# A longer hold on TensorE's tiling in a planned kernel of attention and two dense layers

## The chip, the cores and the metric

The kernel runs on one core of a Trainium2 chip. The metric is the device time of one execution in microseconds (us), the median of several runs. Five engines work in parallel, each through its own instructions in a fixed order: TensorE (PE in the profile, with its weight loads as PEld), VectorE (DVE), ScalarE (ACT), GpSimd (POOL) and SyncE (SP), which issues all the transfers.

## The reference, cut to what matters

The sizes are B, H, S, D = 4, 8, 576, 64 and 2304 tokens through two dense layers, 512 to 2048 and back.

```python
scores = scale * np.matmul(q, k.transpose(0, 1, 3, 2))
x = (psi_rel / psi_i)[..., None]          # log distances, one per pair of positions
h = np.maximum(x @ w1 + b1, 0.0)          # 32 hidden units
bias = h @ w2                             # one value per head
scores = scores + bias.transpose(2, 0, 1)[None, :, :, :]
attn = softmax(scores)                    # over the keys
attn_out = np.matmul(attn, v)
x = attn_out.transpose(0, 2, 1, 3).reshape(B * S, H * D)
h = x @ w_in
out = (h / (1 + exp(-h))) @ w_out
```

All is float32; the kernel makes the precision of the large products out of two parts of each operand (`hi` and `lo`) in a shorter format.

## The kernel before, in words

The program is not written as a loop nest that each engine follows. It is a list of operations, each with the engines that may run it, an estimated cost on each, a due time (`prio`), the buffers that it reads and writes, and a function that emits its instructions. The class `Plan` then walks through simulated time (`order`, lines 118 to 212): whenever an engine is free it takes, among the operations that are ready and whose buffers can be had, the one with the smallest due time. The result is a static order for every engine, and the program emits it. Due times are counted in the plan's own microseconds; they only rank the work.

The work comes in stages that overlap:

- The bias of each pair of positions is computed once for all batches, in 36 tiles (`bias_tile`, line 311): four operations `bias_f` on ScalarE, VectorE or GpSimd (lines 326 and 328), one product `bias_mm` on TensorE (line 334, eight or sixteen matmuls in a 128x32 tiling), one scaling copy `bias_ev` (lines 341 and 343) and a store (line 345). Tiles are due 2.6 apart.
- Attention runs in visits (`visit`, line 463). A visit is one batch, one pair of heads and one or more chunks of 128 query positions. For each chunk (`chunk`, line 537) there are two score products `s_mm` (line 561; the last, half chunk has one, `s_last`, line 552), a maximum on VectorE with the bias added (line 568), the exponential on ScalarE (line 575), two groups of transposes `t_mm` on TensorE (line 584, four and five matmuls) and their copies `p_ev` into the buffer `pt` (on ScalarE or VectorE by the helper `copy`, lines 270 and 272). When all chunks of the visit are in `pt`, the product `pv` (line 483, 20 matmuls in a 128x64 tiling) multiplies them with the values; its result is copied to `xo` and stored to `x_d` (line 497).
- The first batch is done chunk by chunk, 20 visits of one chunk, due 4.5 apart (3.0 for the half chunk); batches 1, 2 and then 3 follow in 24 visits of two and three chunks.
- The dense layers follow in six blocks of 384 tokens with 16 steps each (`ff_step`, line 627): four products `h_mm` (line 633), the gate on ScalarE and VectorE (lines 638 and 642), three products `out_mm` (line 656). Their due times overlap the last three batches of attention; the first block also splits the weights into two parts (lines 352 to 394).

Buffers are scarce and set the order too: `pt` has two, the transposes' two kinds of banks (`TA`, `TB`) one each, the scores' `S`, the bias products' `B` and the outputs' `o` two each.

On TensorE the planner knows three tilings of the array: 1 for `pv`, 2 for `bias_mm`, 0 (the full array) for all else. The table `MODES` names them, `CHANGE` is the time that it adds to the plan for a change, and `KEEP` is added to the due time of every waiting product of another tiling than the present one, when TensorE chooses (lines 58, 168 to 172 and 184 to 186):

```python
wait[e] = [(p + self.KEEP * (self.MODES.get(self.kinds[i], 0) != mode), p, i) for p, i in every]
```

A product of another tiling is taken as soon as no product of the present tiling that could start has a due time up to KEEP later. Until 24 plan-us short products on zeros fill TensorE's idle time (`warm_up`).

Of the kernel before, what the change touches and what calls it, by code (L numbers as in the profile page):

```python
# [46 lines left out]
class Plan:  # L47
# [7 lines left out]
    CALM = 24.0  # L55


    MODES, CHANGE, KEEP = {"pv": 1, "bias_mm": 2}, 0.19, 1.5
    LAG = {"PE": 0.2, "ACT": 0.15, "DVE": 0.13, "POOL": 0.15, "SP": 0.95}

    def __init__(self, caps, banks):
# [726 lines left out]
```

## Time and profile before

| what | value |
|---|---|
| median of three runs | 736.17 us (735.53 to 736.71) |
| the profiled execution | 736.04 us |
| its span, first to last instruction | 734.3 us |
| granted TensorE clock, mean | 0.998 |
| PE busy | 712.6 us, 97% |
| PEld busy | 590.1 us, 80% |
| DVE busy | 421.0 us, 57% |
| ACT busy | 389.4 us, 53% |
| POOL busy | 281.4 us, 38% |

Busy time is the union of an engine's instructions. Matmuls are pipelined, so what a product costs is read from start to start and not from its own duration. In the timeline, neighbouring instructions of one line on one engine are merged into a row: start, time from the first start to the last end, engine, line, operation, destination and source by the program's names, shape, and the count; in square brackets stands the idle time ahead of it and what ended it. A stretch such as "42 to 84 us" is counted from the span's start.

### The profile page before, as it was taken

The page shows a single profiled execution, that of the slowest core. Times are in us where ns is not written, and L with a number is a line of the kernel's source. Part 1 is how long each engine was busy: PE and PEld are TensorE (multiplying, and loading weights), DVE is VectorE, ACT ScalarE, POOL GpSimd, SP SyncE. Part 2 cuts the span into 40 slices and gives each one's busy share as a digit, 9 for nine tenths or more (in the row PEclk, how much of TensorE's full clock was granted, in tenths as well). Part 3 has the DMA queues.
Part 4 walks back from the last instruction along what each step waited for, and adds up shares of the span by engine and source line. Part 5 has one row for each costly group of instructions (what it writes and reads, how often), then busy time and mean ns, then how long its engine had stood idle before and what let it go on. Part 6 is the DMA issues. An engine that isn't in the chain of part 4 may idle for free.

```text
span 734.3 us, 13019 instructions
## 1 busy us (share of the span) xinstructions
PE 712.6 (97%) x4642; PEld 590.1 (80%) x4642; DVE 421.0 (57%) x862; ACT 389.4 (53%) x820; POOL 281.4 (38%) x277
## 2 busy tenths in 40 slices
PE   9899999999999999989999999999999999999997
PEld 4376698677777787778888888899998999999996
DVE  6999968999999999996553544213211221211111
ACT  8899968886786777765443454222222232222222
POOL 5464524474746445573122251123223322422221
PEclk9999999999999999999999999999999999999999
DMA  6998899898584594879856567736454644346001
GB/s 195 372 315 270 277 310 359 278 289 297 191 290 157 203 303 149 272 257 311 293 165 224 168 217 241 263 115 196 148 162 153 186 150 152 125 136 195 1 0 44
DMA packets 68384, 154.77 MB, mean 211 GB/s; under 512 B 9056, under 2 KB 24032, under 8 KB 68320
## 3 DMA queue, kind: packets, MB, share of 16 engines
q1 hardware_dynamic: 68320, 153.94, 63.7%
q8 instruction: 37, 0.61, 0.4%
q14 instruction: 27, 0.22, 0.1%
HBM read 125.12 MB, written 28.79 MB: 210 GB/s over the span
## 4 chain that ended last, share of the span: by engine, by line
PE 46%; issue 7%; DVE 3%; POOL 2%; DMA 1%; ACT 0%; POOLq 0%; DVEq 0%; ACTq 0%
PE psum L633 18%; PE psum L656 18%; PE psum L483 3%; PE psum L561 3%; PE psum L584 3%; POOL M L275 2%; DVE G L568 1%; DVE w L369 1%; DMA G<-in_k_dram 1%; PE psum L552 1%; DVE M L275 0%; DVE w L374 0%; DVE th L642 0%; DVE M L272 0%; DVE w L360 0%
## 5 line engine op out<-in xcount | busy, mean ns | idle before, releaser
L633 PE MATMUL psum<-M,G 128*128 128x384 f32 x1152 | 238.8, 339 | 1.0 <-POOL M L275 0.8
L656 PE MATMUL psum<-G,M 128*128 128x512 f32 x864 | 238.0, 397 | 1.2 <-DVE M L275 0.9
L633 PEld LDWEIGHTS psum<-M,G 128*128 128x128 f32 x1152 | 203.4, 188 | 16.6 <-POOL M L275 1.0
L275 POOL TENSOR_TENSOR M<-th,M 128x384 fp32r<-128x384 f32 x82 | 84.9, 1035 | 272.0 <-ACT M L270 189.3
L642 DVE SCALAR_TENSOR_TENSOR th<-th,psum 128x384 f32<-128x384 f32 x96 | 53.0, 552 | 216.4 <-ACT th L638 216.4
L656 PEld LDWEIGHTS psum<-G,M 128*128 128x128 f32 x864 | 156.7, 188 | 22.2 <-DVE M L275 1.6
L575 ACT ACTIVATE G<-G,sm 128x576 f32<-128x576 f32 (+1 forms) x144 | 111.8, 777 | 53.6 <-DVE sm L568 52.3
L638 ACT ACTIVATE th<-psum 128x384 f32<-128x384 f32 x96 | 47.1, 491 | 161.1 <-PE psum L633 160.0
L568 DVE CUSTOM_DVE_ANT_0 G<-psum,G 128x576 f32<-128x576 f32 (+1 forms) x144 | 106.5, 758 | 27.9 <-PE psum L561 15.5
L584 PE MATMUL psum<-ident,G 128*128 128x128 f32 x656 | 93.5, 276 | 5.7 <-DVE sm L568 3.3
L561 PE MATMUL psum<-G,M 128*128 128x288 f32 x512 | 90.9, 310 | 4.9 <-DVE sm L568 3.5
L584 PEld LDWEIGHTS psum<-ident,G 128*128 128x128 f32 x656 | 75.3, 141 | 23.0 <-issue 4.8
L561 PEld LDWEIGHTS psum<-G,M 128*128 128x128 f32 x512 | 73.9, 190 | 19.7 <-issue 6.7
L483 PE MATMUL psum<-pt,M 128*64 128x128 f32 (+3 forms) x880 | 87.5, 346 | 1.6 <-DVE sm L568 0.8
L483 PEld LDWEIGHTS psum<-pt,M 128*64 128x64 f32 x880 | 52.1, 137 | 30.7 <-issue 6.8
L270 ACT ACTIVATE pt<-psum 128x512 f32<-128x512 f32 (+3 forms) x111 | 59.4, 551 | 28.1 <-PE psum L584 27.0
L275 POOL TENSOR_TENSOR M<-M 64x256 fp32r<-64x256 f32 (+3 forms) x40 | 48.6, 1217 | 57.9 <-DVE M L272 21.0
L270 ACT ACTIVATE M<-th 128x384 fp32r<-128x384 f32 x81 | 42.3, 523 | 40.9 <-DVE th L642 40.0
L272 DVE COPY pt<-psum 128x512 f32<-128x512 f32 (+3 forms) x81 | 45.4, 571 | 21.8 <-PE psum L584 19.1
L275 POOL TENSOR_TENSOR G<-w,G 128x512 fp32r<-128x512 f32 x25 | 35.6, 1425 | 23.8 <-ACT G L270 19.9
L275 POOL TENSOR_TENSOR G<-G 128x576 fp32r<-128x576 f32 x21 | 32.2, 1540 | 29.6 <-PE psum L334 9.6
L326 ACT ACTIVATE G<-lut_sb,cb 128x528 f32<-128x528 f32 (+16 forms) x71 | 41.6, 662 | 0.0
(55 smaller groups left out, 574.1 us busy)
## 6 DMA issues: line engine op xcount, KB each, us to landing
G<-win_d SPq DMA_DIRECT2D x80, 512.0 KB
G<-bias_d SPq DMA_DIRECT2D x48, 576.0 KB
bias_d<-G SPq DMA_DIRECT2D x36, 295.5 KB
G<-in_k_dram SPq DMA_DIRECT2D x16, 576.0 KB
G<-in_w_in_dram SPq DMA_DIRECT2D x16, 512.0 KB
G<-in_w_out_dram SPq DMA_DIRECT2D x16, 512.0 KB
win_d<-G SPq DMA_DIRECT2D x16, 512.0 KB
M<-in_v_dram SPq DMA_DIRECT2D x16, 320.0 KB
```

The source lines that it names most:

```text
L270: A.activation(out=out, in_=in_, func=AF.Copy)
L272: ENG[e].tensor_copy(out=out, in_=in_)
L275: ENG[e].tensor_tensor(out=out, in0=in0, in1=f(in1), op=ALU.subtract)
L483: T.matmul(out=tl(o)[x, 0:w], lhsT=tl(vs)[:, (s + 1) % 5 * 128 + 64 * a:(s + 1) % 5 * 128 + 64 * a + 64], rhs=tl(pt)[:, s + 5 * a if s < 4 ...
L561: T.matmul(out=s[:, hf, 0:288], lhsT=tl(qs)[:, x0 + 128 * a:x0 + 128 * a + 128], rhs=tl(part)[:, S * a + 288 * hf:S * a + 288 * hf + 288], ...
L568: V.tensor_tensor_reduce(out=mine(p, a).rearrange("p (a n) -> p a n", a=2), in0=tl(sps[a]).rearrange("p (a n) -> p a n", a=2)[:, :, 0:widt ...
L575: A.activation(out=mine(p, a), in_=mine(p, a), func=AF.Exp, scale=-1.0, bias=tl(sm)[:, i + a:i + a + 1], accum_out=tl(sq)[:, 2 * c + a:2 * ...
L584: T.transpose(out=tl(tp)[:, 128 * s:128 * s + 128], in_=tl(p)[:, 128 * (s0 + s):128 * (s0 + s) + 128], identity=ident)
L633: T.matmul(out=tl(hp)[:, 0:TB], lhsT=tl(wr)[:, x, 128 * cc:128 * cc + 128], rhs=tl(xs[cc])[:, y, :], start=(cc + m == 0), stop=(cc == NC - ...
L638: A.activation(out=tl(th), in_=tl(hp)[:, 0:TB], func=AF.Tanh, scale=0.5)
L642: V.scalar_tensor_tensor(out=tl(th), in0=tl(th), scalar=1.0, in1=tl(hp)[:, 0:TB], op0=ALU.add, op1=ALU.mult)
L656: T.matmul(out=tl(acc[i]), lhsT=tl(gg)[:, x, 128 * i:128 * i + 128], rhs=tl(wo[fi])[:, y, :], start=(fi == 0 and m == 0), stop=(fi == NF - ...
```

## The change

One constant of the planner is doubled.

```diff
-    MODES, CHANGE, KEEP = {"pv": 1, "bias_mm": 2}, 0.19, 1.5
+    MODES, CHANGE, KEEP = {"pv": 1, "bias_mm": 2}, 0.19, 3.0
```

TensorE's choice now counts a product of another tiling as due 3.0 plan-us later than it is, where it was 1.5. No operation, cost, due time or buffer changes. Since the planner goes on from each choice, the order of later work on all five engines can differ.

## Rows read from the trace of the kernel before

**Rows 1.** The page's totals: busy us, share of span, instructions of each engine.
```profile
PE 712.6 (97%) x4642; PEld 590.1 (80%) x4642; DVE 421.0 (57%) x862; ACT 389.4 (53%) x820; POOL 281.4 (38%) x277
```

**Rows 2.** Stages: stretch, its us, busy us (instructions) per engine, clock, DMA share, GB/s.
```profile
core 0: us, PE busy (x) PEld busy (x) DVE busy (x) ACT busy (x) POOL busy (x), PEclk, DMA share, GB/s
42.00:84.00 42.00, 42.00 (x446) 27.86 (x445) 38.65 (x102) 40.98 (x90) 20.77 (x16) 1.00 0.86 270
84.00:132.00 48.00, 45.82 (x493) 39.41 (x493) 37.83 (x97) 35.69 (x85) 17.52 (x33) 1.00 1.00 333
132.00:320.00 188.00, 177.50 (x1186) 143.29 (x1183) 182.18 (x334) 141.27 (x295) 101.65 (x87) 1.00 0.71 239
320.00:734.00 414.00, 409.08 (x2239) 359.79 (x2237) 126.94 (x265) 137.00 (x286) 117.35 (x117) 1.00 0.52 170
```

**Rows 3.** Timeline of TensorE: products with and without a change of tiling beside them.
```profile
60.77 0.77 PE L561 MATMUL psum<-G,M 128*128 128x288 f32 x4
61.48 1.31 PE L483 MATMUL psum<-pt,M 128*64 128x128 f32 x20
...
97.86 0.77 PE L561 MATMUL psum<-G,M 128*128 128x288 f32 x4
98.47 0.71 PE L584 MATMUL psum<-ident,G 128*128 128x128 f32 x5
...
100.88 1.31 PE L483 MATMUL psum<-pt,M 128*64 128x128 f32 x20
102.12 1.20 PE L584 MATMUL psum<-ident,G 128*128 128x128 f32 x9
103.08 1.30 PE L561 MATMUL psum<-G,M 128*128 128x288 f32 x8
...
104.86 2.40 PE L483 MATMUL psum<-pt,M 128*64 128x128 f32 x40
107.19 1.20 PE L584 MATMUL psum<-ident,G 128*128 128x128 f32 x9
...
152.47 1.15 PE L584 MATMUL psum<-ident,G 128*128 128x128 f32 x9
153.37 1.53 PE L561 MATMUL psum<-G,M 128*128 128x288 f32 x8
```

**Rows 4.** Timeline of TensorE from 48 to 55 us.
```profile
48.02 1.31 PE L483 MATMUL psum<-pt,M 128*64 128x128 f32 x20
49.26 0.66 PE L584 MATMUL psum<-ident,G 128*128 128x128 f32 x4
49.85 1.31 PE L483 MATMUL psum<-pt,M 128*64 128x128 f32 x20
51.09 0.77 PE L334 MATMUL psum<-G,cb 128*32 128x336 f32 x8
51.79 0.77 PE L584 MATMUL psum<-ident,G 128*128 128x128 f32 x5
...
53.55 1.42 PE L334 MATMUL psum<-G,cb 128*32 128x352 f32 x16
54.90 1.31 PE L483 MATMUL psum<-pt,M 128*64 128x128 f32 x20
```

**Rows 5.** Timeline of TensorE from 68 to 73 us.
```profile
68.39 1.31 PE L483 MATMUL psum<-pt,M 128*64 128x128 f32 x20
69.64 0.66 PE L584 MATMUL psum<-ident,G 128*128 128x128 f32 x4
70.22 0.99 PE L334 MATMUL psum<-G,cb 128*32 128x464 f32 x8
71.14 0.77 PE L584 MATMUL psum<-ident,G 128*128 128x128 f32 x5
71.83 1.31 PE L483 MATMUL psum<-pt,M 128*64 128x128 f32 x20
```

**Rows 6.** Timeline of ScalarE: two copies of transposes into the probabilities' buffer.
```profile
47.68 0.71 ACT L270 ACTIVATE pt<-psum 128x640 f32<-128x640 f32 x1
...
65.27 1.19 ACT L270 ACTIVATE pt<-psum 128x512 f32<-128x512 f32 x2
```

## The prediction, made before the changed kernel ran

> **What bounds the kernel now.** I read the profile in this order: the engines' totals, the same engines by stage, then TensorE's timeline inside the stages where the change can act. The totals say that TensorE has matmuls in flight for 712.6 of 734.3 us [rows 1]; the profiled execution took 736.04 us, 1.7 us more than its span and 0.13 us under the median of the runs (736.17), so I work on 736.04 and add 0.13 at the end. The stages say more [rows 2]. From 42 to 84 us TensorE never pauses, but ScalarE is busy for 40.98 of 42.00 us and VectorE for 38.65: three engines are full together. From 84 to 132 us TensorE is the fullest (45.82 of 48.00) and the others have room (VectorE 37.83, ScalarE 35.69), while the DMA share is 1.00. From 132 to 320 us VectorE sets the pace, 182.18 of 188.00 us, and TensorE is idle for 10.5 us. From 320 us on TensorE is alone and full, 409.08 of 414.00 us. So a microsecond of TensorE work that is saved is worth a microsecond at the end after 320 us, nearly that between 84 and 132 us, only in part between 42 and 84 us, and little between 132 and 320 us.
>
> **What the change acts on.** The constant KEEP is added, in the planner's choice for TensorE, to the due time of every waiting product whose tiling is not the one that the array has (lines 168 to 172). Full 128x128 products are tiling 0, the probability-times-value products (`pv`, line 483, 128x64) tiling 1, the bias products (`bias_mm`, line 334, 128x32) tiling 2. The first bias products ended by 90 us and the last `pv` by 467 us, so nothing after that is ordered by it. No instruction is added or removed; what can change is how often TensorE leaves the full tiling and comes back, and in what order all five engines get their static queues.
>
> **What one excursion costs, from rows.** Entry: four score products after transposes take 0.61 us to the next start when a full product follows, and 0.71 us when a `pv` follows [rows 3]: 0.10. Inside: a lone `pv` on one 128-wide chunk takes 100.88 to 102.12, 1.24 us; two in a row, 104.86 to 107.19, take 2.33, so the second cost only 1.09: 0.15 [rows 3]. Exit: nine transposes take 0.96 us after a `pv` (102.12 to 103.08) and 0.90 after a full product (152.47 to 153.37): 0.06 [rows 3]. Together 0.31 us. For a bias product there is one pair, 53.55 to 54.90, 1.35 us for 352 and 368 columns [rows 4]; a lone one of 336 columns takes 0.70 (51.09 to 51.79) [rows 4], and scaling with columns two lone ones would take about 1.50 (an estimate from that row), so 0.15 inside and, with entry and exit as above, again about 0.3. A step from `pv` straight to a bias product (49.85 to 51.09 [rows 4]) saves about half of that.
>
> **How many could go.** Between 42 and 95 us the timeline has 11 groups of `pv` and 15 of bias products, six of them touching, so 20 excursions, 6 us. From 95 to 132 us there are 8 groups with 9 `pv`; after that 24 groups with one `pv` each, due 9.9 plan-us or more apart, which no KEEP of 3 joins. Only the first 132 us can gain. There the plan's own due times decide. Visits of the first batch are due 4.5 apart; `pv` of a visit is due 9.5 after its visit's start (lines 473 and 479), the transposes of the visit after it at 4.5 + 2.6 and 4.5 + 3.2, so a transpose is due 2.4 or 1.8 ahead of the `pv` that it splits from the one before. With KEEP at 1.5 these two differences are larger than the penalty, the transpose wins and TensorE changes twice; at 3.0 they are smaller and the second `pv` goes first, if it is ready. It was ready: at 48.02 a `pv` runs, four transposes at 49.26, the next `pv` at 49.85 [rows 4], whose last input had been copied by 48.39 (47.68 + 0.71) [rows 6]. At 68.39 a `pv` runs, then four transposes, and the next `pv` only at 71.83 [rows 5], though its copies were done at 66.46 (65.27 + 1.19) [rows 6]. A third such pair stands at 90.75 and 93.12. In most other places the second `pv` became ready only after the first had ended. Bias products mostly start within 0.6 to 1.6 us of their last input, so readiness and not the penalty holds them; I count three that a longer hold would let join. Six excursions at 0.3 are 1.8 us gross. The bounds: none (the order changes elsewhere instead), and everything paired, 19 groups of `pv` to 10 (9 x 0.31 = 2.8) and 15 of bias to 10 (5 x 0.27 = 1.35), 4.1 us.
>
> **What of it reaches the end.** About 1.5 of the 1.8 us lie between 42 and 84 us. There ScalarE has only 1.02 us left and VectorE 3.35 [rows 2]; if the planner shifts copies from one to the other they could shrink the stage by the mean, 2.2, if not by 1.0. I take half of the 1.5 us, 0.7. The remaining 0.3 us, at 93, lies where TensorE is the fullest; I count it whole, with the DMA share of 1.00 against it. Sum: 1.0 us earlier.
>
> **What else moves.** A `pv` that waits longer holds its probabilities (two buffers of `pt`) and hands its output later to the copy into `xo` on ScalarE or VectorE and to the store into `x_d`, which stands in SyncE's queue in front of loads of queries, biases and keys. In the middle stage `pv` is held behind up to 1.5 plan-us more of score products and transposes; visits there are due 9.9 or more apart, so `pt` comes free long before it is wanted. Feeding VectorE's maxima ahead of a 2.3 to 2.9 us `pv` could help the engine that sets that stage; at most its idle 5.8 us could be won [rows 2], and a worse order could lose as much. Nothing in the rows favours a sign, so I take 0 and let both ends widen the range. After 320 us the order does not matter while TensorE never waits: 0, with 4.9 us of idle time [rows 2] as the most that it could give. The last `pv` ends 260 us before the end, so its later output delays nothing.
>
> **The rivals.** (1) ScalarE is the real limit from 42 to 84 us. For it: 40.98 of 42.00 us busy [rows 2]. Against it: VectorE had room, and most of the copies can go to either. Then only the join at 93 counts, 0.3 us: 735.9. The Trainium skill, in Perfetto Trace Analysis, section Identifying the Most-Contended Engine, judges ScalarE and VectorE by occupancy but TensorE by its weight loads and not by its matmul time; by that rule ScalarE is the contended engine there and the gain of that stage would be nothing. The trace's 27.86 of 42.00 us of weight loads [rows 2] agree with it, but TensorE's starts leave no gap there, which speaks against it.
> (2) Pairing takes over: once two `pv` are held together, the next two come ready together, and the saving passes on whole. 2 to 4.1 us: about 733.6, from 732.0 to 734.2. For it: the 2.4 and 1.8 lie between the two penalties. Against: readiness.
> (3) Slower: the hold on `pt`. With 3.0 a `pv` is due, in effect, 12.5 after its visit's start, behind both transposes of the visit two later (11.6 and 12.2), and their results can't be copied until that same `pv` has freed its `pt`. With 1.5 it was 11.0, ahead of them. Each time the copy waits for the whole `pv` and a change, 1.24 + 0.10 = 1.3 us, and with it the single bank of transposes, and VectorE and ScalarE, which are full, lose that time. One such visit among the eleven before 95 us eats the gain; with three it is 4.0 - 1.0 = 3.0 us slower: 739.2, range 737 to 740. For it: the buffers' count and the full engines. Against: the planner simulates the copies too, and bias products can fill in.
> That the change does nothing at all can't be: the 2.4 lies between the two constants and ready pairs stand in the trace.
>
> **How the numbers follow.** A measurement of this kernel can tell about 0.2% from no change, 1.5 us: faster means under 734.7, slower over 737.6. The forecast, a gain of 0.2 to 2 us, gets 0.36, of which 0.16 lies under 734.7 and 0.20 within; its time is 736.04 - 1.0 + 0.13 = 735.2. Rival 1 gets 0.12, all within. Rival 2 gets 0.21, all faster. Rival 3 gets 0.31, of which 0.27 slower and 0.04 within. So faster 0.37, same 0.36, slower 0.27. The range runs from the full pairing, 732.0, to the far side of rival 3, 739.8, which leaves out about 0.15.
>
> **What would show it.** In the timeline of TensorE, `pv` in runs of 40 matmuls near 48, 68 and 91 us, and fewer than 20 excursions between 42 and 95 us: the step on joining holds. The last bias product earlier than 90 us by about 0.7, and the first `pv` wider than 128 columns (135.22 us before) earlier by about 1: the gain is kept. The same number of excursions, or as much idle on TensorE behind copies into `pt` as was saved, shows it wrong: a new wait of transposes for copies speaks for rival 3, unchanged times of the last bias product for rival 1. A change of the total that arises between 132 and 320 us, with VectorE's idle time different, would mean that the reordering outweighs what I counted.

## The result and the profile after

The changed kernel takes 743.12 us (median; 741.74 to 745.44) against 736.18 us for the kernel before beside it: a ratio of 1.0098, 95% interval 1.0069 to 1.0127. It is 6.9 us slower; 735.2 was forecast, and the time lies outside the range of 732.0 to 739.8. The profiled execution took 741.74 us, its span is 740.0 us, 5.7 more than before.

The page's totals and then the same four stages, in the kernel after (columns as in [rows 1, 2]):

```profile
PE 712.5 (96%) x4642; PEld 591.5 (80%) x4642; DVE 427.1 (58%) x859; ACT 384.8 (52%) x820; POOL 283.7 (38%) x280
```

```profile
42.00:84.00 42.00, 42.00 (x451) 28.08 (x449) 39.72 (x103) 40.99 (x91) 21.55 (x21) 1.00 0.87 279
84.00:132.00 48.00, 44.81 (x490) 38.83 (x486) 39.37 (x96) 32.09 (x84) 17.31 (x25) 1.00 0.93 299
132.00:320.00 188.00, 175.51 (x1153) 142.24 (x1153) 179.68 (x329) 138.75 (x293) 97.75 (x88) 0.99 0.72 240
320.00:734.00 414.00, 410.97 (x2254) 362.31 (x2251) 131.52 (x265) 137.21 (x287) 122.99 (x123) 1.00 0.52 170
```

TensorE does the same work in 740.0 instead of 734.3 us. The count of its products shows where it falls behind: 451 against 446 up to 84 us and 490 against 493 up to 132 us, so level, but 1153 against 1186 from 132 to 320 us [rows 2]. If every product counts with its usual time from start to start (an estimate from the two traces), TensorE is 1.1 us ahead of the kernel before at 100 us, 0.4 ahead at 140, 2.1 behind at 160, 4.4 behind at 200, only about 1 behind at 260, and 5.2 behind at 360, where it stays. The dense layers have caught up in between: the 96th matmul of line 633 starts at 228.9 us before and at 228.7 after.

The first stages did in part what the change says. TensorE's timeline in the kernel after, pairs of `pv` and the last bias product:

```profile
67.94 2.40 PE L483 MATMUL psum<-pt,M 128*64 128x128 f32 x40
70.28 1.20 PE L584 MATMUL psum<-ident,G 128*128 128x128 f32 x9
...
89.93 1.18 PE L334 MATMUL psum<-G,cb 128*32 128x512 f32 x16
...
93.23 2.40 PE L483 MATMUL psum<-pt,M 128*64 128x128 f32 x40
```

The pair that stood apart in [rows 5] is joined. The `pv` come in the same order in both kernels, so they can be counted off: the pair at 93.23 us is the one that stood at 93.12 and 95.62. The other two pairs that the prediction called ready were not joined: the `pv` at 48.02 and 49.85 us start at 46.62 and 50.91 now, those at 90.75 and 93.12 at 88.69 and 93.23. Between 42 and 95 us there are 14 excursions instead of 20. The joined pair takes 2.34 us (67.94 to 70.28), as read from [rows 3].

Not all of the lead at 100 us is the change's. The profiled execution of the kernel before has a stretch at the lower clock from 35.5 to 38.9 us, ahead of everything that the change moves; the one after has none there (rows in the last section). `late` and `before_sp`, two of the runs below, keep the order of before up to 90 us and have no such stretch either. Their last bias product starts at 88.36 and 88.59 us instead of 88.94, so 0.3 to 0.6 of the 1.1 us come from the clock.

**What is late.** Split at the first dense product, nearly all of the 5.7 us lie ahead of it. This product begins at 155.31 us instead of 149.29, 6.0 later; from there to the end it is 584.7 us, before 585.0. The inputs of that product are the outputs of the first batch times the reciprocals of their row sums: stored to `rec_d` (lines 532, 534), loaded again (608), multiplied (614), split. SyncE's transfers, first in the kernel before, then after:

```profile
134.65 0.62 SPq L532 DMA_DIRECT2D rec_d<-rt  x1
135.32 0.58 SPq L534 DMA_DIRECT2D rec_d<-rt  x1
...
138.48 2.41 SPq L608 DMA_DIRECT2D xp<-rec_d  x4
...
143.97 0.33 SPq L352 DMA_DIRECT2D G<-in_w_in_dram  x1
...
145.81 0.39 SPq L352 DMA_DIRECT2D G<-in_w_out_dram  x1
```

```profile
135.38 1.15 SPq L459 DMA_DIRECT2D G<-bias_d  x2
137.59 0.63 SPq L532 DMA_DIRECT2D rec_d<-rt  x1
138.35 0.60 SPq L534 DMA_DIRECT2D rec_d<-rt  x1
...
140.56 0.40 SPq L352 DMA_DIRECT2D G<-in_w_in_dram  x1
...
142.74 0.33 SPq L352 DMA_DIRECT2D G<-in_w_out_dram  x1
143.12 3.16 SPq L608 DMA_DIRECT2D xp<-rec_d  x4
```

The row sums themselves are there at 134.6 before and 135.0 after (end of their copy into `rt`). Their store goes out 2.9 us later: in the redrawn order it stands behind two loads of biases, which leave SyncE at 136.53, and then waits 1.0 us, which the trace puts down to the transfer of a wide weight. The loads go out 4.6 us later: two wide weights (512 KB each, at 140.56 and 142.74) now stand ahead of them, which stood behind them before. For the first input the last piece of the loads lands at 150.62 us instead of 144.58 (the update of its semaphore), 6.0 later. First GpSimd's multiplication and subtraction of narrowed weights and the dense product in the kernel before, then after:

```profile
144.74 1.02 POOL L614 TENSOR_TENSOR xp<-xp 128x384 f32<-128x384 f32 x1 [1.60 <-DMA xp<-rec_d]
...
149.63 1.75 POOL L275 TENSOR_TENSOR G<-w,G 128x512 fp32r<-128x512 f32 x1
...
149.29 0.68 PE L633 MATMUL psum<-M,G 128*128 128x384 f32 x3
```

```profile
148.81 1.61 POOL L275 TENSOR_TENSOR G<-w,G 128x512 fp32r<-128x512 f32 x1 [2.68 <-ACT G L270]
...
150.84 1.01 POOL L614 TENSOR_TENSOR xp<-xp 128x384 f32<-128x384 f32 x1
...
154.34 1.33 PE L584 MATMUL psum<-ident,G 128*128 128x128 f32 x5 [1.12 <-ACT pt L270]
155.31 3.45 PE L633 MATMUL psum<-M,G 128*128 128x384 f32 x12
```

So the lateness grows from 0.4 (row sums) over 2.9 (store), 4.6 (load issued), 6.0 (load landed) and 6.1 (multiplication) to 6.0 us (product). Each step is read from the traces.

But the load is not alone. In the kernel after, GpSimd's multiplication has no idle time ahead of it. It stands behind a subtraction of narrowed weights that had waited 2.68 us for ScalarE's copy, and behind two short fills; GpSimd comes free at 150.71 us, and the load had landed at 150.62. In the kernel before, that kind of subtraction stands behind the multiplication. So two redrawn orders, SyncE's and that of the narrowing, end within 0.1 us of each other, and in this order an earlier load alone would bring the multiplication forward by 0.1 us at most. The experiments below have a kernel for either case.

### The profile page after: what moved, and what is told of

Its sections match the earlier page's. It is cut to its first block, busy times and chain, and to the rows that moved or that the text cites. A ratio compares the mean times of both kernels' runs of the same rounds, so it can differ in the third digit from the quotient of the medians.

```text
span 740.0 us, 13012 instructions
## 1 busy us (share of the span) xinstructions
PE 712.5 (96%) x4642; PEld 591.5 (80%) x4642; DVE 427.1 (58%) x859; ACT 384.8 (52%) x820; POOL 283.7 (38%) x280
## 4 chain that ended last, share of the span: by engine, by line
PE 68%; DVE 11%; issue 10%; DMA 5%; POOL 3%; ACT 2%; SPq 0%; POOLq 0%; DVEq 0%; ACTq 0%
PE psum L633 20%; PE psum L656 20%; PE psum L483 8%; PE psum L584 8%; PE psum L561 6%; PE psum L334 4%; POOL M L275 2%; PE psum L552 2%; DMA x_d<-xo 2%; DVE G L568 2%; DVE w L369 2%; DVE w L374 2%; DVE w L360 1%; DVE G L275 1%; PE psum L723 1%
## 5 line engine op out<-in xcount | busy, mean ns | idle before, releaser
L275 POOL TENSOR_TENSOR M<-th,M 128x384 fp32r<-128x384 f32 x86 | 90.3, 1050 | 266.7 <-ACT M L270 194.5
L656 PEld LDWEIGHTS psum<-G,M 128*128 128x128 f32 x864 | 157.2, 188 | 23.1 <-DVE M L275 1.9
L561 PE MATMUL psum<-G,M 128*128 128x288 f32 x512 | 88.5, 305 | 4.3 <-DVE sm L568 3.9
L275 POOL TENSOR_TENSOR M<-M 64x256 fp32r<-64x256 f32 (+3 forms) x34 | 41.9, 1234 | 48.5 <-DVE M L272 19.9
L272 DVE COPY pt<-psum 128x640 f32<-128x640 f32 (+3 forms) x75 | 43.9, 594 | 21.3 <-PE psum L584 18.7
L275 POOL TENSOR_TENSOR G<-w,G 128x512 fp32r<-128x512 f32 x29 | 39.7, 1368 | 40.6 <-ACT G L270 34.7
L275 POOL TENSOR_TENSOR G<-G 128x576 fp32r<-128x576 f32 x24 | 37.4, 1572 | 29.0 <-PE psum L334 9.7
L326 ACT ACTIVATE G<-lut_sb,cb 128x384 f32<-128x384 f32 (+16 forms) x68 | 40.3, 663 | 0.0
```

The lines of the kernel that those rows point to most:

```text
L272: ENG[e].tensor_copy(out=out, in_=in_)
L275: ENG[e].tensor_tensor(out=out, in0=in0, in1=f(in1), op=ALU.subtract)
L561: T.matmul(out=s[:, hf, 0:288], lhsT=tl(qs)[:, x0 + 128 * a:x0 + 128 * a + 128], rhs=tl(part)[:, S * a + 288 * hf:S * a + 288 * hf + 288], ...
L656: T.matmul(out=tl(acc[i]), lhsT=tl(gg)[:, x, 128 * i:128 * i + 128], rhs=tl(wo[fi])[:, y, :], start=(fi == 0 and m == 0), stop=(fi == NF - ...
```

## The experiments

All profiled executions are told by two numbers: when the first dense product starts, and how long the program runs from there to the end of its span. They belong to one execution each, which can lie some us from the median (749.7 us for `early`, 743.5 for `lock30_h4`, 748.8 for `after_sp`). The second number is not the same in all orders; it runs from 570.1 to 592.5 us.

| kernel | median us | ratio, 95% | first dense product | from there |
|---|---|---|---|---|
| before | 736.2 | | 149.3 | 585.0 |
| after | 743.1 | 1.0069 to 1.0127 | 155.3 | 584.7 |
| early | 747.6 | 1.0115 to 1.0173 | 156.2 | 591.8 |
| late | 744.0 | 1.0070 to 1.0118 | 151.1 | 591.6 |
| neutral1 | 738.8 | 1.0019 to 1.0044 | 149.6 | 587.1 |
| neutral2 | 745.2 | 1.0083 to 1.0133 | 153.0 | 590.5 |
| pvonly | 742.8 | 1.0058 to 1.0103 | 148.3 | 592.5 |
| biasonly | 738.2 | 1.0010 to 1.0035 | 155.3 | 580.0 |
| joined | 741.7 | 1.0062 to 1.0090 | 154.7 | 584.9 |
| light15 | 723.7 | 0.9800 to 0.9837 | 146.6 | 574.4 |
| light30 | 726.2 | 0.9837 to 0.9878 | 152.1 | 572.0 |
| lightn2 | 722.6 | 0.9797 to 0.9830 | 147.3 | 573.2 |
| lock15_h4 | 742.0 | 1.0054 to 1.0091 | 150.4 | 590.4 |
| lock30_h4 | 738.1 | 1.0014 to 1.0051 | 157.2 | 584.5 |
| after_sp | 747.0 | 1.0131 to 1.0175 | 160.7 | 586.3 |
| before_sp | 735.9 | 0.9989 to 1.0007 | 148.9 | 585.0 |
| light30_sp | 729.3 | 0.9897 to 0.9924 | 156.8 | 570.1 |
| front30 | 742.3 | 1.0055 to 1.0092 | 154.1 | 586.9 |
| front15 | 735.7 | 0.9980 to 1.0001 | 147.7 | 584.8 |
| after_3 | 743.4 | 1.0073 to 1.0104 | 154.8 | 586.3 |

**Is it the longer hold itself, and in which part of the plan?** `early` has 3.0 only for the first 100 plan-us, `late` only after them; `pvonly` and `biasonly` have 3.0 only for choices without and with a bias product.

```diff
+                    keep = 3.0 if now < 100.0 else 1.5      # early; late: the other way round
-                    wait[e] = [(p + self.KEEP * (self.MODES.get(
+                    wait[e] = [(p + keep * (self.MODES.get(
```

> KEEP is 3.0 while the plan's time is under 100 us and 1.5 after it: the longer hold acts on the first batch and the bias alone. Theory A (the loss comes from the longer hold itself in the middle stage, 140 to 345 us): the early gain of about 1 us stays and the middle is as before, 735 to 736 us. Theory B (the loss is not made by the hold at all but by the new order in which VectorE and GpSimd meet in the middle stage, so that any change upstream redraws it): no tie to the 743 or to the 736, anywhere from 733 to 744 us, with the difference from before arising after 140 us and going with VectorE's lengthened instructions. Theory C (the hold on the two probability buffers in the first batch costs): 741 to 744 us, with the loss already there at 130 us.

> KEEP is 1.5 while the plan's time is under 100 us and 3.0 after it, so that the first part is as before and the longer hold acts in the middle stage alone. Theory A: all of the loss, 742 to 744 us. Theory C: nothing of it, 736 us. Theory B: anywhere from 733 to 744 us, with the same tie to VectorE's lengthened instructions.

> The longer hold between the full tiling and that of the probability-times-value products alone; every choice that has to do with bias products keeps 1.5. Theory A: most of the loss, 741 to 744 us, since only these products exist in the middle stage. Theory B: anywhere from 733 to 750 us, the end again 416.5 us after the last narrowing. If the later last bias product (89.93 for 88.94 us) made the loss by way of the loads behind it, the first narrowing is back at about 130 us.

> The longer hold in choices that have to do with bias products alone; between full products and probability-times-value products it stays 1.5. Theory A: 735 to 737 us, since no bias product runs after 90 us. Theory B: anywhere from 733 to 750 us, the end 416.5 us after the last narrowing. If the later last bias product made the loss, the first narrowing is at 133 to 135 us and the time 739 to 744 us.

The halves do not add up: each half alone costs as much as the whole or more (11.0 and 7.5 against 6.9 us), and `early`, which holds no `pv` longer after 100 plan-us, loses its time after 140 us all the same. It is slower than any of its theories allowed. Its trace has four stretches at the lower clock (from 122.8, 187.6, 273.0 and 334.4 us), the one after a single one (154.3 us); at the 1.1 us that this one costs, they would be some 4 of its 11 us, an estimate. `biasonly` starts its dense layers as late as the kernel after and still ends within 2 us of the kernel before, so most of a late start can be won back.

**Is it any redrawing of the order?** Two numbers that have nothing to do with the hold are moved a little, with KEEP at 1.5: the plan's lag of ScalarE (`neutral1`) and its price of a change of tiling (`neutral2`).

```diff
-    LAG = {"PE": 0.2, "ACT": 0.15,
+    LAG = {"PE": 0.2, "ACT": 0.16,
```
```diff
-    MODES, CHANGE, KEEP = {"pv": 1, "bias_mm": 2}, 0.19, 1.5
+    MODES, CHANGE, KEEP = {"pv": 1, "bias_mm": 2}, 0.21, 1.5
```

> KEEP stays 1.5. Only the planner's assumed delay after ScalarE's operations goes from 0.15 to 0.16 us, a number that describes nothing on the chip; it serves to redraw the static orders a little. Theory B (the time is set by how each redrawn order happens to meet VectorE's limit in the middle stage, whatever redraws it): it moves too, by 1 to 10 us either way, with the last narrowing of the weights (line 369 of the kernel before, at 318.1 us there) moved by as much. Theory A (the longer hold itself costs): 735.5 to 737 us.

> KEEP stays 1.5. Only CHANGE, the time that the planner adds for a change of tiling, goes from 0.19 to 0.21 us, again a number of the plan alone. Theory B: it moves by 1 to 10 us either way, the end following the last narrowing at a distance of about 416.5 us as in all runs so far. Theory A: 735.5 to 737 us.

2.3 and 8.0 us slower (excess of the ratio times 736.2). A step of 0.02 us in one of the plan's prices costs about as much as the change under study, so a redrawn order can cost this much without any longer hold. That it is the redrawn order that the change pays for, too, is the likely reading; two neutral orders do not prove it. It is not the clock: at the same mean granted clock, 0.996 and 0.998, the span is 740.0 and 742.2 us in the kernel after, and 734.0 to 735.3 and 734.0 to 736.6 us in the kernel before.

**What is joining worth if no other engine is redrawn?** `joined` takes the order of the kernel before and moves eight groups of products on TensorE alone, between 46 and 92 us, so that each stands right behind the last `pv` or bias product before it. Only the first pair is of one tiling.

> KEEP 1.5 and the plan's order of before, of which only TensorE's own order is changed by hand in eight places between 46 and 92 us: a special product that was ready is put directly behind the special product before it, ahead of the transposes or scores that stood between. All other engines keep their order. Seven excursions fewer. If the price of an excursion is as read and a joined order is kept elsewhere (the first step of the prediction, without the redraw of the plan): one pair of like products saves 0.3 us, six neighbours of unlike tiling 0.15 to 0.2 us each, 1.2 to 1.5 us in all, of which up to half stays in the full first stage; 734.5 to 736 us. If joining itself costs (the hold on the probability buffers): 738 us or more, with the loss there at 95 us.

Its timeline of TensorE, its wait of ScalarE's copies from 55 to 100 us, and that wait in the kernel before (`joined` has its lines 31 further down):

```profile
47.52 2.53 PE L514 MATMUL psum<-pt,M 128*64 128x128 f32 x40
49.98 0.66 PE L615 MATMUL psum<-ident,G 128*128 128x128 f32 x4
51.39 0.77 PE L365 MATMUL psum<-G,cb 128*32 128x336 f32 x8 [0.75 <-ACT pt L301]
...
ACT pt L301 <- PE psum L615: 5.8, 3, 2.4
```

```profile
ACT pt L270 <- PE psum L584: 1.4, 3, 0.8
```

Here the price is like that of rival 3, by a wait next to the one that it named: the copies do not wait for `pv` to free its buffer, but for transposes (line 615) that stand behind the second `pv`. That is 4.4 us more on ScalarE, and TensorE is some 5 us behind at 100 us. The dense layers start 5.4 us late and the rest is as long as before. In the kernel after the planner moved the other engines along, and this wait grew by 1.0 us only.

**Is it VectorE beside GpSimd?** In all of these kernels GpSimd's subtractions of the low parts are replaced by fills of zeros: in the order of before (`light15`), of after (`light30`) and of `neutral2` (`lightn2`).

```diff
     def sub(e, out, in0, in1):
+        if e == "POOL":
+            G.memset(f(out), 0.0)
+            return
         ENG[e].tensor_tensor(
```

> The kernel before with its static order unchanged, but each subtraction that GpSimd runs is replaced by a memset to zero of the same destination, so the low parts that GpSimd makes are left out; all other work and every order is as before. GpSimd then reads no memory in these places and is done sooner. Theory B: VectorE's instructions get back their short durations, some 40 us of VectorE time in the middle stage, and the time falls by 5 to 15 us, to 721 to 731. Theories A and C: VectorE's time is no matter for the difference; the time falls only by what waits for GpSimd, 0 to 3 us.

> The changed kernel with its static order unchanged, and the same subtractions on GpSimd replaced by memsets to zero (the low parts that GpSimd makes are left out). Theory B: the gap of 7 us to the other order shrinks to within 2 us of the same kernel with KEEP 1.5, and may turn its sign, since the first part gained 1 us. Theories A and C: the gap stays at 5 to 7 us.

> The kernel with CHANGE 0.21 and KEEP 1.5 (745.2 us), its orders unchanged, with the subtractions on GpSimd replaced by memsets to zero (the low parts that GpSimd makes are left out). If what a redrawn order costs is made by its meetings of VectorE and GpSimd, the 8.9 us between this order and that of before shrink to under 3 us: 723 to 726.5 us beside 723.7. If it is made by other waits, it stays at 6 to 9 us: 730 to 733.

Two of VectorE's groups by line, the narrowing's last two steps (lines 369 and 374), in the kernel before, after and in `light15` (three lines further down):

```profile
L369 DVE SCALAR_TENSOR_TENSOR w<-G,w 128x512 uint32<-128x512 uint32 x32 | 32.0, 1001 | 0.4
L374 DVE SCALAR_TENSOR_TENSOR w<-G,w 128x512 uint32<-128x512 uint32 x32 | 28.3, 886 | 0.1
```

```profile
L374 DVE SCALAR_TENSOR_TENSOR w<-G,w 128x512 uint32<-128x512 uint32 x32 | 32.1, 1004 | 0.1
L369 DVE SCALAR_TENSOR_TENSOR w<-G,w 128x512 uint32<-128x512 uint32 x32 | 30.3, 946 | 0.2
```

```profile
L377 DVE SCALAR_TENSOR_TENSOR w<-G,w 128x512 uint32<-128x512 uint32 x32 | 23.3, 728 | 0.1
L372 DVE SCALAR_TENSOR_TENSOR w<-G,w 128x512 uint32<-128x512 uint32 x32 | 22.8, 712 | 0.4
```

The same instruction takes 0.71 to 0.73 us on average without the subtractions and 0.89 to 1.00 with them. The three orders become 12.5, 17 and 22.6 us faster, and what they need from the first dense product on draws together: 572.0 to 574.4 instead of 584.7 to 590.5. So GpSimd's subtractions have a large part in what an order costs, most clearly in `neutral2`, whose 8.0 us are gone. How they do it is not separated: a fill is also shorter on GpSimd itself (128x512 takes 0.54 us on average in `light15`, the subtraction 1.43 before). The start of the dense layers stays apart, 146.6 and 152.1, 5.5 us, nearly as in the full kernels (a stretch at the lower clock from 120.1 us in `light30` is a part of it); so this lateness is not made by GpSimd's subtractions. At the end 2.5 of the 6.9 us remain, since this order is the quicker one afterwards. In `light30` it is the load that is late, for GpSimd has long been free (line 614 is three lines further down):

```profile
148.92 1.20 POOL L617 TENSOR_TENSOR xp<-xp 128x384 f32<-128x384 f32 x1 [5.06 <-DMA xp<-rec_d]
```

In `light15` the same multiplication starts at 140.71 us.

**Can the plan be taught?** `lock15_h4` and `lock30_h4` give the planner a model in which these instructions of VectorE and GpSimd exclude each other, with KEEP at 1.5 and 3.0.

> KEEP 1.5, but the planner now counts a VectorE operation that has all operands in SBUF as starting only after a GpSimd operation that is under way, and the other way round, takes shorter costs for four steps of the narrowing, and lets VectorE prefer work on PSUM while GpSimd is busy. If the meetings of the two engines are what the plan gets wrong, VectorE's lengthening in the middle stage falls by a third or more and the time by 3 to 10 us: 726 to 733. If the order is only redrawn once more: 737 to 747.

> The same planner with KEEP 3.0. If a plan that knows of the meetings keeps its gain on the chip, the two constants are within 2 us of each other, at 725 to 733. If the order is only redrawn: 737 to 747, with no tie to the other.

742.0 and 738.1 us (ratios 1.0054 to 1.0091 and 1.0014 to 1.0051): neither beats the kernel before.

**Is it the first load of wide weights?** The first narrowing of weights starts 3.7 us later in the kernel after (134.1 against 130.4), and in SyncE's order the store of an output stands ahead of the first wide load. `after_sp` puts the first three wide loads and a load of queries ahead of that store (the fourth stays right behind it), `before_sp` puts the wide loads behind it in the kernel before, `light30_sp` is the first edit in `light30`.

```diff
+    FRONT = [("ld_wide", 0), ("ld_q", 23), ("ld_wide", 1), ("ld_wide", 2), ("st_x", 15),
+             ("ld_wide", 3), ("st_rec", 0), ("st_rec", 1), ("st_x", 16)]   # after_sp: SyncE's order here
```

> The changed kernel with one stretch of SyncE's order put as before: the first four loads of wide weights no longer stand behind the store of an output that is not ready until 119.9 us; that store and two stores of row sums stand behind them instead. All other engines keep the order of the changed kernel. Theory S (the late first load starts the narrowing of the weights 3.7 us late and this comes back at the end): the first narrowing at 130 to 131 us instead of 134.1, the last one about 3 us earlier, 739.0 to 740.5 us, a ratio of 1.004 to 1.006. Theory M (the orders lose in the middle whatever the first load does, because VectorE is held up there): the first narrowing is earlier but the last one is not, 742.0 to 744.0 us, 1.008 to 1.010.

> The kernel before with the same stretch of SyncE's order put as in the changed kernel: a store that becomes ready at about 120.7 us, two stores of row sums and a second store stand ahead of the first wide loads. All other engines keep the order of the kernel before. Theory S: the first narrowing at 133 to 134 us instead of 130.4, the last one and the end about 3 us later, 739 to 740 us, a ratio of 1.004 to 1.005. Theory M: the narrowing catches up in the middle stage, 736 to 737 us, 1.000 to 1.001.

> The changed order with GpSimd's subtractions replaced by fills of zeros (the low parts are left out), and with the wide loads ahead of the store as above. Theory S: the 2.5 us between the two orders without GpSimd's subtractions is this late load, so 723.5 to 724.5 us, a ratio of 0.983. Theory M: 725.5 to 727 us as without the edit, 0.986.

Theory S fell. In `before_sp` the first wide load goes out 1.9 us later (119.3 against 117.4), the first narrowing still starts at 130.0 us, and the time stays. In `after_sp` the edit did not reach its aim: the first wide load goes out at 120.5 as without it, and it is the moved store that is paid for. ScalarE and TensorE in `after_sp` (lines 21 further down):

```profile
130.17 0.22 ACT L291 ACTIVATE xo<-psum 128x64 f32<-128x64 f32 x1 [4.99 <-DMA x_d<-xo]
...
130.44 0.48 PE L546 MATMUL psum<-ident,sq 128*128 128x128 f32 x1 [4.00 <-ACT xo L291]
```

A copy into `xo` waits 5.0 us for a store to free its buffer. From there to 190 us nearly every instruction of VectorE runs 5.3 to 6.0 us later than the same one in the kernel after, and the span is 7.0 longer; by the medians it is 3.9. Both theories are missed, as in `light30_sp`, where the same copy waits 4.6 us and the time is 3.2 us above `light30`. TensorE stood for 4.0 and 4.2 us there, and in both traces its clock is the lower one from within that pause (127.7 and 125.3 us), which is a part of the loss. So what SyncE's order delays at 125 us is for the most part not won back.

**Is it the early collisions?** Up to the last narrowing (318.1 us before, 322.4 after) VectorE's account is: idle 25.9 and 25.5 us, work 238.7 and 238.4, lengthening 53.5 and 58.5 (an instruction's time over the tenth percentile of its line and shape). 3.7 of the 5.0 us more lie between 42 and 132 us. The idle time is equal only in sum: up to 132 us it is 20.2 and 17.2, from there to the last narrowing 5.8 and 8.3. `front30` and `front15` fill zeros for the subtractions of that stretch alone, in the order of after and of before; `after_3` for three of them in the order of after.

```diff
+        if e == "POOL":
+            n = count[0]
+            count[0] += 1
+            if n in (18, 23, 25):            # after_3; front30: 7 <= n <= 25
+                G.memset(f(out), 0.0)
+                return
```

> The changed kernel; of GpSimd's subtractions only those between 42 and 132 us (19 of 191) are fills of zeros instead, so their low parts are left out; the rest stays. In this stretch VectorE's instructions are lengthened beside GpSimd by 7.4 us in the changed kernel and by 3.7 before. Theory E (the early collisions, which are 3.7 of the 5.0 us of additional lengthening up to the last narrowing, carry the loss): 739 to 740.5 us, and 3 to 4.5 us above front15. Theory M (the collisions after 132 us carry it): 742 to 743.5 us, about 7 above front15.

> The kernel before with the same done to its order (21 of 189 subtractions between 42 and 132 us are fills, their low parts left out). Both theories: little, since only about 1.7 us of lengthening beside subtractions goes, 0.96 of it after 95 us: 734.5 to 736.3 us.

> The changed kernel with three single subtractions on GpSimd, those at 99.1, 122.3 and 130.3 us, replaced by fills (these three low parts are left out). Beside them three instructions of VectorE are lengthened by 1.1, 1.0 and 0.7 us, 2.8 together. Theory E: VectorE passes its delays on whole, so 740 to 741 us. Theory M: they are taken up by its idle time, 742.3 to 743.5 us.

Theory E fell. In `front15` the dense layers start 1.6 us earlier and the span is 1.7 shorter, but 0.6 of this is there at 48 us already, from the clock of the execution before; by the medians it is 0.9, and the interval includes no gain at all. In `front30` VectorE is 2.35 us ahead of the kernel after at 132 us; 1.05 us of this goes at 137 us, to an instruction of 1.63 instead of 0.55 us beside GpSimd, and at 152.5 it is level. GpSimd and VectorE in `front30` (lines eight further down):

```profile
151.26 1.00 POOL L622 TENSOR_TENSOR xp<-xp 128x384 f32<-128x384 f32 x1 [1.81 <-DMA xp<-rec_d]
...
151.61 1.07 DVE L622 TENSOR_TENSOR xp<-xp 128x384 f32<-128x384 f32 x1 [0.81 <-DMA xp<-rec_d]
```

Both engines now stand and wait for the loads of `rec_d`, which go out at 143.59 us as in the kernel after (143.12), behind the same two wide weights: what the narrowing had gained ends at these loads. `after_3` is the other case. Here the loads land early, at 149.30 and 149.47 us for the first input where it was 150.44 and 150.62, and no engine waits for them. GpSimd in `after_3`:

```profile
148.99 1.38 POOL L283 TENSOR_TENSOR G<-w,G 128x512 fp32r<-128x512 f32 x1 [2.88 <-ACT G L270]
...
150.75 1.05 POOL L622 TENSOR_TENSOR xp<-xp 128x384 f32<-128x384 f32 x1
```

The multiplication starts 0.1 us earlier than in the kernel after, since the subtraction of narrowed weights still stands ahead of it. So either delay alone holds the dense layers: the narrowing in `after_3`, the load in `front30` and `light30`, both in the kernel after. No run has both of them moved in the kernel after.

## Why the prediction was wrong

**The count of excursions held in number, and the part of their price that can be read.** Six were to go and six went (20 to 14); the joined pair costs 2.34 us, 2.33 was read. That the number fits is partly luck: of the three pairs that were to be seen near 48, 68 and 91 us only the one at 68 was joined, and most excursions did not go by joining like with like: `pv` stands in 9 groups instead of 11, the bias products in 16 instead of 15, and 11 groups now touch one of the other kind where six did. By the price's own parts an excursion that ends in a touch saves entry and exit, 0.16, and not the 0.15 inside: 6 x 0.16 + 1 x 0.15 = 1.1 us, where six at 0.3 were 1.8 gross.

**The gain of the first stages held in size, not in its signs.** TensorE was 1.1 us ahead at 100 us, of which 0.3 to 0.6 belong to the clock of the execution before; so 0.5 to 0.8 us of that sum were kept. 1.0 was forecast, as the part kept of a gross that was too large. The last `pv` on a 64-column chunk starts 1.4 us earlier (130.21 against 131.60). The first `pv` wider than 128 columns comes 3.1 us earlier (132.16 against 135.22), where about 1 was named as a sign. But the last bias product comes 1.0 us later (89.93 against 88.94), not 0.7 earlier. Rival 1, no gain from the full stage, does not fit; nor does rival 2, which wanted more.

**Rival 3 had the sign and not the place.** A wait like it is real where the other engines' orders are kept (`joined`), at a price of 5.6 us at the end, where three such visits were put at 4.0. In the kernel after ScalarE's and VectorE's waits for transposes grew by 1.0 and 0.5 us between 55 and 100 us (2.4 and 1.9 against 1.4 and 1.4), and TensorE gained time there.

**The step that failed is "What else moves".** It took the redrawn order after 132 us at 0, between a gain and a loss of 5.8 us, since "nothing in the rows favours a sign". Two things were wrong in it. First the size: VectorE's idle time bounds a gain, not a loss; the loss was 5.7 us by the spans and 6.9 by the medians, with up to 11.0 in other orders. Second, the place: the start of the dense layers was not looked at. SyncE's queue was named (the store of the output in front of loads) and given no price; its order made the load of the first dense input land 6.0 us later, and the order of the narrowing on GpSimd held that input as long. The range did not even reach up to the loss that was allowed, 736.2 - 1.0 + 5.8 = 741.0. And the sentence that a change between 132 and 320 us would outweigh the count was the right one to look at: of ten orders that were drawn anew (the kernel after and nine of the others: early, late, the neutral, split and lock pairs, joined), none was faster than the one before. So a zero with equal ends was the wrong price for a redraw; why all ten are slower is not shown. Where the changed order falls among them could not be read from the profile of before.

**What stays open.** The lateness of 6.0 us is followed through the trace to two delays, each of which `front30` or `after_3` shows to be enough, but it is not undone in any run. That it is also what the end pays for is not shown: in `biasonly` the same lateness goes with a loss of 2 us at most, and in the kernel after TensorE is nearly level again at 260 us before it falls back. In other orders the loss stands elsewhere: `late` and `pvonly` start the dense layers 1.8 us later and 0.9 earlier and need 6.6 and 7.5 us more from there. For these the traces show more idle time on VectorE between 132 us and the last narrowing (11.7 and 11.3 us against 5.8, and 8.3 in the kernel after), and not a single place.

## What to carry to other kernels

In a kernel whose order is planned, a change of the plan's rule has two effects: its own, which can be priced from rows (here about 1 us), and that of a new order on all engines, which can be ten times as large (up to 11.0 us here); draw two or three orders with neutral changes before you put the difference down to the rule. Price the one-sided risk of a stage that has no slack from the chain into the next stage: look for the transfers that the next stage's first product needs, and for what may come to stand ahead of them in the queue. Then look for the second input of that product that is nearly as late: moving one of the two gains nothing. And set profiled executions side by side only with their clocks, stretch by stretch.

## What the runs showed of the hardware

VectorE's instructions that read and write only SBUF get longer beside GpSimd's: the long ones end only after GpSimd's instruction has ended. VectorE and GpSimd in the kernel after:

```profile
155.66 1.75 POOL L275 TENSOR_TENSOR M<-M 64x704 fp32r<-64x704 f32 x1 [0.16 <-PE psum L584]
...
155.79 2.17 DVE L369 SCALAR_TENSOR_TENSOR w<-G,w 128x512 uint32<-128x512 uint32 x1
...
163.09 0.68 DVE L369 SCALAR_TENSOR_TENSOR w<-G,w 128x512 uint32<-128x512 uint32 x1
```

GpSimd's ends at 157.41, VectorE's at 157.96, one usual duration of 0.68 us less 0.13 after it: it had waited. Over the span this is 62.1 us before and 68.2 after, in 73 and 84 instructions longer by over 0.15 us, and all of them lie beside one of GpSimd's. The Trainium skill, in SBUF — State Buffer, section Who interferes with whom, describes this as an exclusive lock on a port pair that the two engines share, in which an operation with two SBUF inputs contends with GpSimd's reads but not with what only writes; the fills of zeros in `light15` agree (18.0 us), though they are also shorter.

TensorE's clock fell after idle time at one place in the middle of the kernel after. TensorE had stood for 0.69 and 1.12 us just before the first dense product; in the stretch that follows the granted clock is 0.50, the lower of its two levels, 1.2 instead of 2.4 GHz (columns as in [rows 2]):

```profile
154.40:157.60 3.20, 3.20 (x12) 3.20 (x13) 3.20 (x3) 2.94 (x7) 2.77 (x3) 0.50 0.99 375
```

Twelve dense products take 3.45 us there and 2.38 at 171.59 us, so the lower clock cost 1.1 us. Idle time alone does not decide it. Around 30 to 36 us the two kernels have the same products and the same three pauses (0.42, 1.12 and 0.99 us), and of these two executions the clock fell only in the one before. First the kernel before, then after, the eight products behind the last pause and the stretch:

```profile
35.64 2.29 PE L561 MATMUL psum<-G,M 128*128 128x288 f32 x8 [0.99 <-DVE sm L568]
35.50:39.00 3.50, 3.36 (x16) 2.92 (x20) 3.44 (x11) 2.37 (x7) 2.48 (x3) 0.51 1.04 396
```

```profile
35.60 1.47 PE L561 MATMUL psum<-G,M 128*128 128x288 f32 x8 [0.99 <-DVE sm L568]
35.50:39.00 3.50, 3.40 (x28) 2.60 (x29) 3.50 (x11) 3.50 (x10) 2.48 (x3) 1.00 1.04 396
```

At 48 us the kernel before is some 0.6 us behind `front15`, which has no such stretch; this is as large as what the change gained.
